# A planned attention and FFN kernel: weight differences and some products and casts also allowed on VectorE, and a new order table

## The chip, the cores and the metric

One core of a Trainium2 chip runs the kernel. The metric is the device time of one execution in microseconds, and lower is better. Before the change three timed runs gave 291.61, 292.24 and 292.89 us, a median of 292.24 us. Engines are called by the profile's names: PE is TensorE, DVE is VectorE, ACT is ScalarE, POOL is GpSimd, and SP is SyncE, which here only issues transfers.

## The reference

Linear attention with exponential features runs on 8 batches of 8 heads (576 tokens, head dimension 64, 128 features), and a maxout FFN takes its output as 4608 tokens of 512 columns.

```python
proj = einsum('bhsd,df->bhsf', x, w_phi)                 # for q and for k
proj = proj - max(abs(proj), axis=-1, keepdims=True)
phi  = concatenate([exp(proj), exp(-proj)], axis=-1)
kv   = einsum('bhsf,bhsd->bhfd', phi(k), v);  z = sum(phi(k), axis=2)
attn = einsum('bhsf,bhfd->bhsd', phi(q), kv) / (phi(q) . z + 1e-6)
x    = attn.transpose(0, 2, 1, 3).reshape(4608, 512)
out  = maximum(maximum(x @ w1, x @ w2), x @ w3) @ w_out
```

## The kernel before

**Units.** The attention is cut into 16 units (half a batch, four heads each). For a unit POOL issues the loads of q (L373) and k (L378) into a `qk_bf` buffer as bf16, and SP those of v (L413) and of the last 64 q tokens of each head, the tail (L405). POOL casts the tail into the same buffer (L408). Units 0 to 3 are transposed by PE; from unit 4 on SP issues two transposing transfers `qkT<-qk_bf` (L454), one for q (8 blocks) and one for k with the tail (10 blocks). PE projects (L474, L572, L579), DVE takes the maxima (L478), ACT the exponentials (L482, L563, L582). POOL multiplies v with a correction from the maxima into `vab` (L527), PE sums `kvps` (L546), PE forms `psn` (L603, L608), DVE adds the two halves into `y` (L614, L617) and takes the reciprocal of the last column (L619), and POOL multiplies the two into `x_sb` (L620, three pieces a unit). From unit 2 on SP issues one transposing transfer `xT<-x_sb` (L639) per unit, and units 0 and 1 are turned by PE (L632).

**FFN.** Nine chunks of 512 tokens follow the units: chunk b needs the turned x of units 2b and 2b+1, the last chunk the tails of all units. The kernel computes max(xw1, xw2, xw3) w_out as max(0, x(w2-w1), x(w3-w1)) w_out plus x(w1 w_out). For this, six weight differences (L739, three column pieces of each of two matrices, `dst - w_bf[0]`, 128x1024 bf16) are made once, and the product w1 w_out is made by PE into `pm` (L760). A chunk then has 12 groups of four products `ups` (L660), ReLU by ACT or DVE (L673, L675), the maximum by DVE (L669), and four row blocks `ops` of four products x(w1 w_out) (L692) and six with `hT` (L697), copied by ACT or DVE (L705) and stored by SP or ACT (L709).

**The order.** Nothing decides the order at run time. Each piece of work is a node with its engine's cost, made in the order of the program text, and the string PLAN lists all 1562 nodes as `number engine buffer-slots @ start`. `plan` gives each node that engine, those slots and that place; `fill` sorts by start and puts products with no use (`idler`, L802) into PE's early gaps. Each engine then works strictly in its order, and SP's and POOL's queues do so too: a transfer that waits holds up all that its engine issues after it. Transfers issued by SP and ACT use eight semaphores in turn, so one waits until the one eight places ahead of it has landed. The cost of a node names the engines on which the planner may put it.

Of the kernel before, what the change touches and what calls it, by code (L numbers as in the profile page):

```python
# [19 lines left out]
P = 128  # L20
# [14 lines left out]
BY_PE = 4  # L35
# [54 lines left out]
109T0@9.7 24T5@10.2 48D@10.4 192G@10.8 21D@10.7 46A@11.3 129T74@10.5 30T23@11.2 110D@11.0 45A@11.5 133D1@11.6 31A@11.8 32A@12.3 115T60@11.8  # L90
120A1@12.7 337S0@8.8 189G@11.0 62G0@11.8 36D@12.0 25D@12.5 33D@12.9 119A1@13.2 1163G@11.9 49T14@13.0 51D@13.5 61G@12.7 35A@13.7 60G@13.7
265G@14.8 122T52@13.6 125D1@14.1 34A@14.2 121D@14.7 55A@14.7 66T43@14.9 57G@15.1 1166G@16.2 50D@15.3 117A@14.9 130A@15.3 56G@16.9 118D@15.9
132D@16.5 127A@15.6 126A@16.1 123A@16.5 82A0@17.0 128D@16.8 131A@17.1 124A@17.4 1165G@18.0 58G@18.8 144A1@17.9 271T0@15.6 140A@18.1 146G1@18.9
272D2@17.4 116A@18.3 267T1@16.0 147G@20.0 69T27@17.6 268D@17.6 143G@20.1 262G@20.3 67D0@18.2 142G@21.0 72A@18.7 335G0@22.1 141G@22.8 79T0@17.9
73A@19.2 280T51@18.3 68D@18.4 71A@19.7 286D0@18.8 111T4@18.7 63T36@19.2 112D@19.4 1164G@23.9 134T74@20.1 405G1@24.6 145G@25.4 80A0@20.2 81A@20.4
64A@20.7 70A@20.9 336G@26.5 164T0@20.9 283D@20.0 65A@21.3 135D@20.6 137T37@21.3 136D@21.2 285A0@21.5 198T2@21.6 139D@21.8 199A3@22.0 138D@22.3
88T64@21.9 83T27@22.5 89D0@22.9 284A0@22.2 282A@22.7 166A1@23.2 165A@23.4 84D1@23.4 196T1@22.9 281A@23.7 154T36@23.6 158A1@24.2 156A@24.7 90D@23.9
157A1@25.1 93T02@24.0 85D@24.4 94D2@24.8 167A1@25.6 1177T5@24.5 194T4@25.0 155A@25.7 148T70@25.5 1178D0@25.3 95D@25.9 159T65@26.1 195A@26.2 161A@27.1
91D0@26.3 86D1@26.4 87G0@27.2 1173T3@26.4 150A1@27.6 149D@26.5 162A@27.7 197D@26.7 92G@27.9 338G@28.7 1174D@27.3 96D2@27.9 151T27@27.0 273T41@27.6
153A@28.2 276D@28.0 152A@28.4 1175T0@27.9 168T37@28.5 98T2@28.9 1176D@28.6 163A@28.5 169D1@29.2 277A@29.0 100T5@29.2 341S0@33.6 170D@29.8 193S3@34.9  # L100
101D@30.3 1181T0@29.3 97G@28.9 160A@29.5 274A@29.9 173T36@30.6 102T7@31.0 275A@30.4 178T54@31.2 1182A@30.9 279D@30.6 174D0@31.2 99D@31.7 207T03@31.8
171D1@31.9 103A@31.4 278A@31.8 1170G@30.8 287T72@32.1 175D@32.0 212A1@32.2 176D0@32.7 289A@32.7 288A@33.0 1183T1@32.4 209A@33.2 291D0@32.8 179D2@33.1
200T62@33.8 208A1@33.7 408S0@35.5 290D@33.6 211A@34.2 172G1@32.9 183T5@34.1 1179T7@34.3 1184D@33.9 475S1@36.1 201A@34.7 180D@34.5 177G@33.7 204A@35.2
185T1@35.6 210D1@35.0 1171G@34.4 181D2@35.6 269T4@35.8 182G@36.5 213D@35.7 202A@35.6 184D@36.3 1168G@37.3 1185T0@36.2 186D@36.6 205A@36.1 270A@36.6
187T3@37.5 1167G@39.4 1186A@37.7 206D@36.8 305T51@37.8 203D@37.4 214T24@38.0 307A0@38.2 188D@38.0 306A0@38.7 219T60@38.4 217D@38.3 1205T3@38.7 308A@39.2
406S2@37.6 1180D@38.7 309A@39.7 220D1@39.3 221D@39.9 1193T5@39.6 218D@40.5 298A0@40.1 225A1@40.3 340S@41.6 266S1@44.4 228A0@40.5 339S2@45.0 1194A1@40.6
216A@41.1 1206D@41.3 1195T7@40.4 222T61@41.4 215A@41.4 224D@41.9 237T04@41.6 1169G@41.5 295T52@41.8 240A1@42.0 1172G@43.6 239A1@42.5 227G@45.7 407G@47.8
238A@43.0 297D@42.5 1207T3@42.2 241A@43.5 301A1@43.9 296D@43.1 1191T1@43.0 1199T2@43.9 1196A@44.1 1192A@44.5 226G@48.0 223D@43.7 310T05@44.8 232T46@45.1
1208D@44.7 292T71@45.3 404G@50.1 311A@45.3 293D@45.7 473G3@50.8 312A@45.7 294D@46.3 1197T3@45.6 235A@46.2 1189T0@46.5 1190D@47.5 233A@46.7 314A@47.2
318A0@47.7 236A@47.8 245A1@48.2 1200A@48.3 242T7@47.3 1198D@48.1 1211T1@47.4 1212D@49.0 1203T0@48.3 1201T6@49.2 300G@51.5 234A@48.8 356T32@50.1 313A@49.3  # L110
# [142 lines left out]
def kernel(  # L253
# [480 lines left out]
    for i in range(2):  # L734
        for h in range(JT // 2):
            c = slice(2 * P * h, 2 * P * (h + 1))
            def diff(n_, i=i, c=c):
                dst = w_bf[i + 1]
                nc.gpsimd.tensor_tensor(dst[:, :, c], dst[:, :, c], w_bf[0][:, :, c], ALU.subtract)  # L739
            n_ = node("wd", 0, {"POOL": 2.1}, None, [w_nodes[0], w_nodes[i + 1]], [], port=True)  # L740
            diffs[i].append([chosen(n_, diff)])
# [92 lines left out]
```

## Time and profile before

| what | value |
|---|---|
| median of three timed runs | 292.24 us (291.61 to 292.89) |
| the profiled execution | 290.7 us |
| its span, first to last instruction | 288.7 us |
| PE busy | 272.4 us, 94% |
| DVE, ACT, POOL busy | 210.6, 199.2, 157.3 us |
| bytes moved | 44.06 MB |

PE counts as busy while a product is under way. Its clock is the share of full speed that it was granted. "issue" as a cause of a wait means that nothing in the profile explains it, and a chain row gives start, duration and work of one piece of the chain that ended last. A row of the timeline ends with the idle time ahead of it and what ended that.

### The profile page before, as it was taken

How to read it: one execution, taken by the hardware profiler on the slowest of the kernel's cores; microseconds unless marked ns; L12 is line 12 of the kernel's file. 1: busy time of each engine (PE TensorE's matmuls, PEld its weight loads, DVE VectorE, ACT ScalarE, POOL GpSimd, SP SyncE). 2: the span in 40 equal slices, each digit the busy share in tenths (PEclk: the TensorE clock that was granted, in tenths of full speed). 3: DMA queues.
4: the chain of work that ended last, by engine and by line, in shares of the span. 5: the costliest groups of instructions: out<-in, count | busy, mean ns of one | idle time of the engine just before them, and what ended most of it. 6: DMA issues, size and time to landing. Idle time of an engine off the chain costs nothing.

```text
span 288.7 us, 8420 instructions
## 1 busy us (share of the span) xinstructions
PE 272.4 (94%) x3432; PEld 150.8 (52%) x3432; DVE 210.6 (73%) x428; ACT 199.2 (69%) x472; POOL 157.3 (54%) x171
## 2 busy tenths in 40 slices
PE   8879999999997949999999999999998999999993
PEld 5557654665554524564555655565455544444541
DVE  3999988999987864885999869989977513155510
ACT  4899999898996773689997998897876220321010
POOL 5699999999726960495178349361982500000000
PEclk9999999999999996999999999999999999999999
DMA  7999999999999999979906399996152330120234
GB/s 161 281 202 209 208 258 258 154 218 154 191 185 232 240 162 283 156 166 182 166 5 167 60 155 242 170 199 141 37 120 86 97 85 0 39 109 36 52 132 109
DMA packets 74678, 44.06 MB, mean 153 GB/s; under 512 B 51152, under 2 KB 65808, under 8 KB 74640
## 3 DMA queue, kind: packets, MB, share of 16 engines
q1 hardware_dynamic: 57296, 27.37, 45.9%
q0 software_dynamic: 14912, 11.77, 28.9%
q10 hardware_dynamic: 2432, 4.39, 4.1%
q8 instruction: 27, 0.44, 0.6%
q14 instruction: 11, 0.09, 0.1%
HBM read 34.64 MB, written 9.44 MB: 153 GB/s over the span
## 4 chain that ended last, share of the span: by engine, by line
PE 72%; DMA 12%; POOL 7%; ACT 3%; issue 2%; SPq 1%; DVE 1%; POOLq 0%; DVEq 0%; ACTq 0%
PE ups L660 30%; PE ops L697 14%; PE ops L692 10%; PE kvps L546 5%; PE psn L603 5%; DMA xT<-x_sb 4%; DMA v_raw<-in_v_dram 3%; POOL vab L527 3%; DMA qkT<-qk_bf 3%; PE psk L474 2%; PE psm L572 2%; DMA tail_raw<-in_q_dram 2%; PE psq L474 2%; ACT Ek L482 2%; PE psn L608 1%
## 5 line engine op out<-in xcount | busy, mean ns | idle before, releaser
L660 PE MATMUL ups<-xT,w_bf 128*128 128x512 bf16 x432 | 104.0, 385 | 4.2 <-DMA xT<-x_sb 4.2
L527 POOL TENSOR_TENSOR vab<-v_raw,em 128x1152 bf16<-128x1152 f32 (+1 forms) x36 | 68.7, 1911 | 22.3 <-DMA qkT<-qk_bf 8.3
L482 ACT ACTIVATE Ek<-psk 128x512 bf16<-128x512 f32 x128 | 73.9, 640 | 6.3 <-PE psk L474 4.0
L563 ACT ACTIVATE Eq<-psm 128x512 bf16<-128x512 f32 x128 | 71.7, 630 | 7.5 <-PE psm L572 6.2
L660 PEld LDWEIGHTS <-w_bf 128*128 128x128 bf16 x432 | 40.1, 99 | 49.6 <-issue 7.2
L620 POOL TENSOR_TENSOR x_sb<-y,rden 128x384 bf16<-128x384 f32 x48 | 38.9, 824 | 38.9 <-DVE rden L619 28.6
L697 PE MATMUL ops<-wout_bf,hT 128*128 128x512 bf16 (+2 forms) x222 | 52.0, 373 | 0.0
L669 DVE TENSOR_TENSOR hT<-hT,ups 128x512 bf16<-128x512 bf16 x54 | 35.5, 681 | 17.1 <-PE ups L660 15.8
L478 DVE TENSOR_REDUCE mk<-psk 128x4 f32<-128x512 f32 x64 | 42.6, 681 | 4.5 <-PE psk L474 2.1
L478 DVE TENSOR_REDUCE mq<-psq 128x4 f32<-128x512 f32 x64 | 41.5, 683 | 4.5 <-PE psq L474 4.3
L673 ACT ACTIVATE hT<-ups 128x512 bf16<-128x512 f32 x40 | 24.9, 634 | 23.6 <-PE ups L660 21.9
L705 ACT COPY osb<-ops 128x512 f32<-128x512 f32 x23 | 13.6, 596 | 37.0 <-PE ops L697 37.0
L697 PEld LDWEIGHTS <-hT 128*128 128x128 bf16 x222 | 20.7, 98 | 22.8
L614 DVE TENSOR_TENSOR y<-psn,sq 128x390 f32<-128x390 f32 x48 | 26.3, 556 | 4.4 <-PE psn L603 2.2
L617 DVE TENSOR_TENSOR y<-y,psn 128x390 f32<-128x390 f32 x48 | 26.3, 556 | 2.4 <-DVE y L614 0.5
L474 PEld LDWEIGHTS <-qkT 64*128 64x128 bf16 x576 | 18.8, 94 | 16.4 <-issue 11.1
L603 PEld LDWEIGHTS <-Eq 128*128 128x128 bf16 x512 | 21.9, 98 | 10.4 <-issue 3.1
L603 PE MATMUL psn<-kv_sb,Eq 128*128 128x65 bf16 x512 | 24.1, 194 | 1.9 <-issue 1.8
L692 PE MATMUL ops<-xT 128*128 128x512 bf16 x96 | 24.6, 380 | 0.0
L675 DVE TENSOR_SCALAR hT<-ups 128x512 bf16<-128x512 f32 x14 | 9.3, 685 | 20.7 <-PE ups L660 20.7
L546 PE MATMUL kvps<-vab,Ek 64*128 64x65 bf16 x1152 | 21.8, 191 | 1.7 <-issue 1.2
L546 PEld LDWEIGHTS <-Ek 64*128 64x128 bf16 x1152 | 20.3, 95 | 2.9 <-issue 1.4
(70 smaller groups left out, 280.6 us busy)
## 6 DMA issues: line engine op xcount, KB each, us to landing
v_raw<-in_v_dram SPq DMA_DIRECT2D x14, 576.0 KB, 6.2
out_dram<-osb SPq DMA_DIRECT2D x20, 256.0 KB, 3.6
qk_bf<-in_k_dram POOLq DMA_DIRECT2D x15, 288.0 KB, 6.6
qk_bf<-in_q_dram POOLq DMA_DIRECT2D x15, 256.0 KB, 6.6
out_dram<-osb ACTq DMA_DIRECT2D x12, 256.0 KB, 2.4
w_bf<-in_moe_w_dram POOLq DMA_DIRECT2D x3, 768.0 KB, 11.6
v_raw<-in_v_dram ACTq DMA_DIRECT2D x2, 576.0 KB, 6.7
tail_raw<-in_q_dram SPq DMA_DIRECT2D x32, 32.0 KB, 5.3
```

Source lines behind the costliest of these rows:

```text
L474: nc.tensor.matmul(ps[s]()[:, i, :], lhsT=qkT()[r, n, :], rhs=wph[r, :], start=True, stop=True)
L478: return nd(kind, {"DVE": 0.598 if n == 4 else 0.331}, lambda: nc.vector.tensor_reduce(dst(m()), ps()[:, 0:n, :].rearrange("p (a j) f -> p ...
L482: return nd("ek", {"ACT": 0.478 if n == 4 else 0.264}, lambda: nc.scalar.activation(dst(Ek[g]()), ps()[:, 0:n, :], EXP, scale=1.0 - 2.0 * ...
L527: made.append(chosen(n_, lambda n_, g=g, t0=t0, t1=t1: (nc.vector if n_.eng == "DVE" else nc.gpsimd).tensor_tensor(vab()[:, g, t0:t1, 0:D] ...
L546: nc.tensor.matmul(kvps[ab]()[:, pr, g, :], lhsT=Ek[g]()[r, t, :], rhs=vab()[r, g, t, :], start=(pr == prs[0] and g + j == 0), stop=(pr == ...
L563: return nd("eq", {"ACT": 0.478 if n == 4 else 0.264}, lambda: nc.scalar.activation(Eq[g]()[:, t0:t0 + n, :], ps()[:, 0:n, :], EXP, scale= ...
L603: nc.tensor.matmul(o, lhsT=Eq[g]()[:, 8 * (c % 2) + 4 * pr + 2 * ab + c // 2, :], rhs=kv()[:, pr, ab, g, :], start=True, stop=True)
L620: divs.append(nd("x", {"POOL": 0.767}, lambda th=th, y=y, rden=rden: nc.gpsimd.tensor_tensor(x_sb()[:, 6 * th:6 * th + 6, :], y()[:, :, 0: ...
L660: nc.tensor.matmul(ups(), lhsT=w_bf[i + (not plain)][:, ct, j * P:(j + 1) * P], rhs=tokens_of(ct), start=(ct == 0), stop=(ct == CT - 1))
L669: nc.vector.tensor_tensor(dst, dst, src, ALU.max)
L692: nc.tensor.matmul(ops_()[:, 0:hi - lo], lhsT=tile_of(ct, tt), rhs=line_w(c_i > MOVE, ct, lo, hi), start=(ct == 0), stop=False)
L697: nc.tensor.matmul(ops_()[:, 0:hi - lo], lhsT=hT()[:, j, tt * P:(tt + 1) * P], rhs=wout_bf[:, j, lo:hi], start=plain and j == 0, stop=(j = ...
```

## The change

Four kinds of nodes may now stand on another engine, and the table is a new one: the planner that made it weighed each order also in two cases in which transfers take longer. The table has the same 1562 nodes. Of what is newly allowed it uses this: two of the six weight differences, three of 48 multiplications into `x_sb` (two of unit 1, one of unit 3) and two of 16 casts of tails go from POOL to DVE. All 36 products of v stay on POOL. Several nodes that had a choice of engine already also change sides: 21 instead of 14 ReLUs and 21 instead of 16 copies of `kvps` are on DVE, 12 instead of 7 small casts L531 and all four copies of `pm` are on ACT. PE has the same products, and 46 instead of 44 idlers. New line numbers lie two or three above the old ones from L527 on.

```diff
 PLAN = """
-14S0@0.8 1D@0.8 3G@1.2 0G@1.6 4A@1.1 5A@1.8 10G0@2.2 16D@4.0 15A@4.0 11S@1.3 ...
...
-        n_ = nd("C", {"POOL": 0.233}, None, [n_t], [t_raw, qk_b], port=True)
+        n_ = nd("C", {"POOL": 0.24, "DVE": 0.13, "ACT": 0.17} if by_pe else {"POOL": 0.24}, None, [n_t], [t_raw, qk_b], port=True)
...
                 costs = {"POOL": 0.128 + 0.1074 * (t1 - t0)}
+                if u < BY_PE:
+                    costs["DVE"] = 0.064 + 0.0667 * (t1 - t0)
...
-            divs.append(nd("x", {"POOL": 0.767}, lambda th=th, y=y, rden=rden: nc.gpsimd.tensor_tensor(
+            n_ = nd("x", {"POOL": 0.767, "DVE": 0.464} if by_pe else {"POOL": 0.767}, None, [n_], [y, rden, x_sb], port=True)
+            divs.append(chosen(n_, lambda n_, th=th, y=y, rden=rden: (nc.vector if n_.eng == "DVE" else nc.gpsimd).tensor_tensor(
...
-                nc.gpsimd.tensor_tensor(dst[:, :, c], dst[:, :, c], w_bf[0][:, :, c], ALU.subtract)
-            n_ = node("wd", 0, {"POOL": 2.1}, None, [w_nodes[0], w_nodes[i + 1]], [], port=True)
+                (nc.vector if n_.eng == "DVE" else nc.gpsimd).tensor_tensor(dst[:, :, c], dst[:, :, c], w_bf[0][:, :, c], ALU.subtract)
+            n_ = node("wd", 0, {"POOL": 2.1, "DVE": 0.64}, None, [w_nodes[0], w_nodes[i + 1]], [], port=True)
```

**SP, around the turning of x of units 4 and 5.** In the rows of before, `qk_bf_1429` belongs to unit 7, `qk_bf_1716` to unit 8, `qk_bf_1949` to unit 9, `x_sb_1999` to unit 4 and `x_sb_2275` to unit 5; a block of 8x128 is q, one of 10x128 is k.

```order
L454 DMA_TRANSPOSE qkT_1697<-qk_bf_1429 128x10x128
L709 DMA out_0_dram<-osb_1752 128x512
L413 DMA v_raw_1961<-in_v_dram 128x2x576
L709 DMA out_0_dram<-osb_1693 128x512
L454 DMA_TRANSPOSE qkT_1983<-qk_bf_1716 128x8x128
L709 DMA out_0_dram<-osb_1427 128x512
L413 DMA v_raw_2063<-in_v_dram 128x2x576
L454 DMA_TRANSPOSE qkT_2142<-qk_bf_1949 128x10x128
L454 DMA_TRANSPOSE qkT_1983<-qk_bf_1716 128x10x128
L413 DMA v_raw_2266<-in_v_dram 128x2x576
L639 DMA_TRANSPOSE xT_75<-x_sb_1999 128x9x128
L639 DMA_TRANSPOSE xT_75<-x_sb_2275 128x9x128
```

After the change, on the same stretch of SP, unit 7 is `qk_bf_1049`, unit 8 `qk_bf_1718`, unit 9 `qk_bf_1810`, and the x of units 4 and 5 are `x_sb_2133` and `x_sb_2295`.

```order
L454 DMA_TRANSPOSE qkT_1920<-qk_bf_1718 128x8x128
L454 DMA_TRANSPOSE qkT_1380<-qk_bf_1049 128x10x128
L413 DMA v_raw_2010<-in_v_dram 128x2x576
L711 DMA out_0_dram<-osb_1645 128x512
L454 DMA_TRANSPOSE qkT_2030<-qk_bf_1810 128x8x128
L405 DMA tail_raw_2126<-in_q_dram 64x2x64 x2
L711 DMA out_0_dram<-osb_1664 128x512
L454 DMA_TRANSPOSE qkT_1920<-qk_bf_1718 128x10x128
L454 DMA_TRANSPOSE qkT_2030<-qk_bf_1810 128x10x128
L405 DMA tail_raw_2251<-in_q_dram 64x2x64 x2
L641 DMA_TRANSPOSE xT_75<-x_sb_2133 128x9x128
L641 DMA_TRANSPOSE xT_75<-x_sb_2295 128x9x128
```

Unit 8's q now stands ahead of unit 7's k, unit 9's q has moved up into this stretch, and of three v loads one is left.

**POOL, the loads in the same stretch.** `qk_bf_2465` is unit 11, `qk_bf_2495` unit 12, `qk_bf_1869` unit 10, and `x_sb_2275` unit 5, in the rows of before.

```order
L620 TENSOR_TENSOR x_sb_2275<-y_2185,rden_2261 128x384
L620 TENSOR_TENSOR x_sb_2275<-y_2218,rden_2284 128x384
L620 TENSOR_TENSOR x_sb_2275<-y_2258,rden_2286 128x384
L527 TENSOR_TENSOR vab_2215<-v_raw_1431,em_2204 128x18x64
L378 DMA qk_bf_1869<-in_k_dram 128x2x576
L527 TENSOR_TENSOR vab_2368<-v_raw_1961,em_2348 128x18x64
L373 DMA qk_bf_2465<-in_q_dram 128x4x256
L373 DMA qk_bf_1949<-in_q_dram 128x4x256
L378 DMA qk_bf_2495<-in_k_dram 128x2x576
```

After the change `x_sb_2295` is unit 5, `tail_raw_2251` the tail of unit 10, and `qk_bf_2406`, `qk_bf_2443` and `qk_bf_2461` are units 10, 12 and 11.

```order
L529 TENSOR_TENSOR vab_2185<-v_raw_1495,em_2176 128x18x64
L533 CAST vab_2185<-em_2176 128x36
L623 TENSOR_TENSOR x_sb_2295<-y_2262,rden_2280 128x384
L623 TENSOR_TENSOR x_sb_2295<-y_2229,rden_2293 128x384
L623 TENSOR_TENSOR x_sb_2295<-y_2174,rden_2316 128x384
L408 CAST qk_bf_2406<-tail_raw_2251 128x2x64
L378 DMA qk_bf_2406<-in_k_dram 128x2x576
L373 DMA qk_bf_2406<-in_q_dram 128x4x256
L378 DMA qk_bf_2443<-in_k_dram 128x2x576
L373 DMA qk_bf_2461<-in_q_dram 128x4x256
```

The second product of v of unit 6 now stands ahead of x of unit 5 instead of behind it. All loads behind x wait for a cast, and the cast for the tail that SP issues just ahead of x. Unit 9's q load has left this stretch.

**POOL, the loads ahead of unit 7's k transposition.** In the rows of before the loads are those of unit 7's k, unit 8's q, unit 10's q, unit 8's k and unit 9's k.

```order
L378 DMA qk_bf_1429<-in_k_dram 128x2x576
L527 TENSOR_TENSOR vab_1734<-v_raw_980,em_1728 128x18x64
L373 DMA qk_bf_1716<-in_q_dram 128x4x256
L373 DMA qk_bf_1869<-in_q_dram 128x4x256
L378 DMA qk_bf_1716<-in_k_dram 128x2x576
L378 DMA qk_bf_1949<-in_k_dram 128x2x576
```

After the change five loads stand behind one another.

```order
L373 DMA qk_bf_1718<-in_q_dram 128x4x256
L378 DMA qk_bf_1049<-in_k_dram 128x2x576
L373 DMA qk_bf_1810<-in_q_dram 128x4x256
L378 DMA qk_bf_1810<-in_k_dram 128x2x576
L378 DMA qk_bf_1718<-in_k_dram 128x2x576
```

Unit 10's q load has left this place, and unit 9's q load has come to it. Unit 7's k is now second in the row, behind unit 8's q.

More of the change, by code (lines that the diff above doesn't have):

```diff
@@ L90 @@
[L90 to L93, printed above, removed]
@@ L196 @@
[L196 to L197 removed]
+11S0@0.8 1D@0.8 4A@1.1 0G@1.2 14S@1.3 3G@1.7 5A@1.8 17S0@1.9 9G0@2.2 2G@2.9 105G1@3.1 106S1@3.5 104G@3.8 12A@4.0
+7A@4.3 13A@4.6 6A@4.9 191S2@5.1 20T0@5.1 21D0@5.8 30T12@6.3 337S3@6.7 34A0@6.7 33D0@6.7 15A@7.2 16D@7.3 31A@7.5 36D@7.5
```

221 lines of the change are left out of this document (111 added, 110 removed).

## The prediction

> **What bounds the kernel now.** I read the page first (busy time, slices, chain by engine), then windows of one slice each.
>
> ```profile
> PE 272.4 (94%) x3432; PEld 150.8 (52%) x3432; DVE 210.6 (73%) x428; ACT 199.2 (69%) x472; POOL 157.3 (54%) x171
> PE   8879999999997949999999999999998999999993
> PEclk9999999999999996999999999999999999999999
> PE 72%; DMA 12%; POOL 7%; ACT 3%; issue 2%; SPq 1%; DVE 1%; POOLq 0%; DVEq 0%; ACTq 0%
> 86.40:93.60 7.20, 5.47 (x58) 2.95 (x58) 5.24 (x14) 4.88 (x13) 4.62 (x5) 1.00 1.31 242
> 100.80:108.00 7.20, 3.67 (x62) 2.26 (x59) 4.54 (x11) 6.01 (x14) 4.66 (x6) 0.94 1.53 157
> 108.00:115.20 7.20, 6.53 (x98) 3.18 (x99) 2.85 (x6) 2.06 (x5) 0.21 (x1) 0.59 1.18 285
> 216.00:223.20 7.20, 5.95 (x90) 3.76 (x84) 5.24 (x13) 4.36 (x13) 1.47 (x3) 1.00 0.20 75
> ```
>
> PE has no gap from about 30 us to the end but for three holes. In a window row the first pair is PE's busy time, and behind the five pairs come the granted clock and DMA's share. The holes lie at 86 to 94, 101 to 115 and 216 to 223 us; in the middle one the clock falls to 0.59. PE's work is the same before and after, so the change can pay only in these holes and lose only by new ones or a later start. All else PE hides.
>
> The chain of waits through the middle hole, with a row of full speed from further on:
>
> ```profile
> 76.83 9.48 DMA v_raw<-in_v_dram
> 86.38 2.13 POOL vab L527
> 88.51 1.28 SPq L454
> 89.89 7.90 DMA qkT<-qk_bf
> 97.88 10.75 DMA xT<-x_sb
> 108.67 4.42 PE ups L660 x10
> 169.65 3.45 PE ups L660 x16
> ```
>
> PE stood still before the first products of chunk 2, which need x of units 4 and 5, and the transfer of unit 5 was issued at 97.88 us and took 10.75. Then ten products took 4.42 us; at 3.45/16 = 0.216 each they take 2.16.
>
> ```profile
> L660 PE MATMUL ups<-xT,w_bf 128*128 128x512 bf16 x432 | 104.0, 385 | 4.2 <-DMA xT<-x_sb 4.2
> L572 PE MATMUL psm<-qkT,wph 64*128 64x512 bf16 x2 | 0.6, 604 | 0.0
> DMA to landing us min/median/max: 3.2/3.5/10.8
> ```
>
> **Hole 1, worth 6.8 us**: 4.2 of wait, 4.42 - 2.16 = 2.26 of slow products, and some 0.3 for the other products that the slow clock caught (two took 604 ns each). The median landing of such a transfer is 3.5 us, the largest is this one.
>
> ```profile
> 88.13 0.22 PE L603 MATMUL psn<-kv_sb,Eq 128*128 128x65 bf16 x2 [1.81 <-issue]
> 217.34 0.23 PE L546 MATMUL kvps<-vab,Ek 64*128 64x65 bf16 x3 [1.25 <-issue]
> q8 instruction: 27, 0.44, 0.6%
> ```
>
> **Holes 2 and 3, 1.81 and 1.25 us**, stand inside a node (ahead of the last two of twelve `psn` products, of the last three of 72 `kvps` products), where no data can be missing. The profile names no releaser. The instruction queue q8 has 27 transfers, one per 254 of PE's 2 x 3432 loads and products, so I take these for late instructions: once behind full DMA queues (share 1.31), once in a dense run, where two sums `kvps` follow each other.
>
> **Why the x transfer was late**, from the timelines of SP and POOL:
>
> ```profile
> 73.67 1.61 SPq L454 DMA_TRANSPOSE qkT<-qk_bf  x1
> 78.74 6.17 SPq L454 DMA_TRANSPOSE qkT<-qk_bf  x1
> 87.20 6.83 SPq L454 DMA_TRANSPOSE qkT<-qk_bf  x2
> 96.08 5.25 SPq L639 DMA_TRANSPOSE xT<-x_sb  x2
> L639 SPq DMA_TRANSPOSE xT<-x_sb x14: 1242/1306/3448, 62.1 to 230.6; - x14
> 86.38 2.12 POOL L527 TENSOR_TENSOR vab<-v_raw,em 128x1152 bf16<-128x1152 f32 x1 [5.17 <-DMA v_raw<-in_v_dram]
> 95.53 0.76 POOL L378 DMA_DIRECT2D qk_bf<-in_k_dram  x1
> 98.66 1.55 POOL L373 DMA_DIRECT2D qk_bf<-in_q_dram  x2
> 100.19 0.72 POOL L378 DMA_DIRECT2D qk_bf<-in_k_dram  x1
> ```
>
> SP was held at its transposing transfers (6.17 and 6.83 us; the median of a turning's issue is 1.31), and once x of unit 5 was out, four loads of POOL, issued from 95.53 to 100.91, moved beside it.
>
> **The change part by part.**
>
> *(a) The order of transfers around x of units 4 and 5: -6.8 us.* After the change the four loads behind x stand behind a cast that needs the tail of unit 10, and SP issues that tail just ahead of x. So they cannot start early; unit 9's q load, one of the four, has left, and unit 10's q load, which had left the front, has come instead. Unit 7's product of v, which led up to them, no longer stands between. The second product of v of unit 6, which stood between x of unit 5 and the loads, now stands ahead of x: 2.13 us, the vab row of the chain. POOL has room for it: it waited 5.17 us for v just before. What must come true is little: at the same issue, the transfer is in time at 10.75 - 4.2 = 6.5 us, against a median of 3.5. Above, SP is held no less than before: it has one transposition more ahead of x and two v loads fewer. Bounds: 0, if transfer and issue are as late as now, and -6.8, if both are as the median has it. I take -6.8, the end that the median is nearer to.
>
> ```profile
> v_raw<-in_v_dram SPq DMA_DIRECT2D x14, 576.0 KB, 6.2
> ```
>
> Late next is unit 7's v load, which SP now issues behind x of unit 5 (it stood nine places ahead of it): some 1.3 us of issue, 6.2 to landing and two products of 2.13 are 11.8 us to its `kvps`, less the 3.5 to 6.5 us that x is under way when chunk 2 begins. That leaves 5.3 to 8.3 us, in which PE has chunk 2's first groups and projections to do; its price is in rival 1.
>
> *(b) Hole 2: -0.9 us.* Whether an instruction block is late depends on DMA traffic about 7 us ahead of its use. The traffic there changes, but does not become small. Bounds -1.81 and 0, and I take the middle, having no row nearer. The Trainium skill (Runtime: NRT & Kernel Launch, section Instruction fetch mechanics) says that crossing an instruction block is mostly hidden. By that rule hole 2 was something else, this term is 0 and the time 0.9 us higher; the rows with 1.81 and 1.25 us inside a node do not agree with it.
>
> *(c) Hole 3: 0.* Units 14 and 15 still have their `kvps` one behind the other. Bounds -1.25 and +1.25.
>
> *(d) Differences, x and casts on DVE, and the front: +1.0 us.*
>
> ```profile
> L739 POOL TENSOR_TENSOR w_bf<-w_bf x6: 2117/2126/2129, 31.0 to 44.1; 128x1024 bf16<-128x1024 bf16 x6
> L753 DVE COPY hT<-pwT 128x1024 bf16<-128x1024 bf16 x3 | 2.0, 681 | 0.0
> L669 DVE TENSOR_TENSOR hT<-hT,ups 128x512 bf16<-128x512 bf16 x54 | 35.5, 681 | 17.1 <-PE ups L660 15.8 <-ACT hT L673 0.8
> L620 POOL TENSOR_TENSOR x_sb<-y,rden 128x384 bf16<-128x384 f32 x48 | 38.9, 824 | 38.9 <-DVE rden L619 28.6 <-issue 6.3 <-DMA qkT<-qk_bf 3.9
> L617 DVE TENSOR_TENSOR y<-y,psn 128x390 f32<-128x390 f32 x48 | 26.3, 556 | 2.4 <-DVE y L614 0.5
> L660 PE MATMUL ups<-xT,w_bf x432: 377/379/631, 39.8 to 270.9; 128*128 128x512 bf16 x144
> L802 PE MATMUL idler<-idle 128*128 128x256 bf16 x44 | 8.6, 322 | 1.2 <-DVE idle L328 1.1
> ```
>
> POOL gives up 2 x 2.13 + 3 x 0.82 = 6.7 us and two casts. DVE takes two differences, each between 0.68 (a copy of the same size) and 1.36 (twice the two-operand row of half the size), and three x at about 0.56: 3.0 to 4.4 us. `ups` waited for x alone (the 4.2 above), never for a difference, so earlier differences gain nothing: the lower bound is 0. DVE is behind ACT's and PE's work there with idle time of its own. What can cost is a difference that now waits behind DVE's maxima: at most one old difference exposed, 2.13 us. Two more idlers in PE's early gaps (0.64 us of filling) say that the front is somewhat looser. I take the middle, 1.0.
>
> *(e) The other nodes with a new side* (ReLUs, copies): DVE at 73% and ACT at 69% are not on the path but by PE's waits: 0, with the cover that PE always has a product ready.
>
> Sum: -6.8 - 0.9 + 1.0 = -6.7. The profiled execution, 288.7 + 2.0 around its span = 290.7, becomes 284.0. It lies 1.5 below the median of the timed runs, 292.24, so I carry the difference over: 292.24 - 6.7 = 285.5 us.
>
> **The rivals.**
>
> *1. x comes late again, but less.* SP is in order and as full as before, and the transfer of unit 5, or behind it the v load of unit 7, then misses by about 2 us (the 8.3 above against some 6 of work). A wait of 1.81 us did not lower the clock (1.00 in the window at 86.40), so only those 2.0 are lost: 287.5.
>
> *2. The change does not do what it says.* The hole stays whole, because the transposing transfers hold SP as now: 285.5 + 6.8 = 292.3, no change that can be measured. For it: SP's 6.17 and 6.83. Against: the loads behind x are chained to x's own neighbour.
>
> *3. Slower: unit 7's k transposition.*
>
> ```profile
> qkT<-qk_bf SPq DMA_TRANSPOSE x1, 10.6
> 89.88 0.28 PE L474 MATMUL pst<-wph,qkT 64*128 64x128 bf16 x4
> ```
>
> It was issued at 73.67 and landed 10.6 us later, at 84.3; PE began unit 7's projections at 89.88, of which 1.81 was hole 2. So it has 89.88 - 84.3 - 1.8 = 3.8 us to spare. Now unit 8's q stands ahead of it on SP, and five loads in a row ahead on POOL. If it lands over 3.8 us later, PE waits; if it is later by another 4, as in the present hole, the clock falls too. Price: a hole like the present one, 6.8, and x 2.0 late behind it on the same queue: 285.5 + 6.8 + 2.0 = 294.3. For it: one transposition behind another was held 6.17 us. Against: in the table of before it was also among four loads.
>
> *4. DVE and POOL block each other.* Two differences and three x on DVE read two operands from SBUF; before, DVE's large two-operand work (L614, L617, L669) always read one from PSUM. If such an instruction waits for a POOL one, a difference comes 2.13 us later, and so may the first `ups`: 287.6. The Trainium skill (SBUF — State Buffer, section Who interferes with whom) says exactly this of VectorE instructions with two SBUF inputs against GpSimd ones that read SBUF; no run here shows it yet.
>
> **How the numbers follow.** The forecast of 285.5 has a chance of 0.50, rival 1 of 0.17, rival 2 of 0.13, rival 3 of 0.16, rival 4 of 0.04. About 0.5% (1.5 us) is what a measurement of this kernel can tell from no change. Faster by more: 0.50 + 0.17 + 0.04 = 0.71; same 0.13; slower 0.16. The range is 283.4 to 293.8: the low end is the forecast with hole 2 and 3 both gone (-0.9, -1.2), the high end takes in rival 2 with the full front of (d), and leaves out more than half of rival 3. The forecast's own range is 283.4 to 287.
>
> **What would show it.** (a) is right if no wait of `ups` for xT over 1 us remains and the clock stays at 1.00 from 30 us to the end; if it stays below 1 in a slice, rival 2 or 3 holds, and the chain says by `xT` or by `qkT` ahead of `psk`, `pst` or `psq`. (b) shows as "issue" waits of PE inside a node near 88 us, (c) near 217 us. (d) shows as waits of `pm` or `ups` for differences or copies between 27 and 50 us, or a first `ups` after 40.8 instead of 39.8; rival 4 as DVE differences over 1.4 us. The prediction is wrong if PE has a new hole elsewhere, most likely before the `kvps` of unit 7.

## The result and the profile after

| | before | after |
|---|---|---|
| median of 15 timed runs | 291.15 us (289.43 to 295.10) | 291.23 us (290.08 to 309.77) |
| ratio after/before | | 0.9998, 95% interval 0.9972 to 1.0025 |
| profiled execution, span | 290.7, 288.7 us | 290.72, 288.6 us |

No difference that can be measured; 285.5 us had been forecast. Two of the 15 runs after the change lie at 306.79 and 309.77 us, and the runs of some kernels below also fall into two groups: all ratios compare the lower group alone.

The page after the change, the same rows as before: busy time, PE's slices, its clock, and the chain by engine.

```profile
PE 271.3 (94%) x3434; PEld 150.0 (52%) x3434; DVE 219.3 (76%) x439; ACT 198.8 (69%) x473; POOL 150.7 (52%) x159
PE   7697988999996899999999999999999999999994
PEclk9979999999999999999999999999999999999999
PE 66%; DMA 10%; DVE 9%; ACT 6%; issue 4%; POOL 3%; SPq 1%; ACTq 0%; POOLq 0%; DVEq 0%
```

The middle hole with its half clock and the hole near the end are gone. In their place stand a looser front (the first seven slices) and a new hole in slices 13 and 14. DVE, which had 1% of the chain before, has 9% of it. The windows of the three old holes and of the new one:

```profile
36.00:43.20 7.20, 5.77 (x68) 3.08 (x65) 7.19 (x14) 5.45 (x13) 7.19 (x7) 1.00 1.17 250
86.40:93.60 7.20, 4.50 (x84) 2.69 (x76) 4.70 (x9) 5.68 (x15) 5.67 (x6) 1.00 1.20 124
93.60:100.80 7.20, 6.13 (x61) 3.06 (x62) 4.84 (x11) 2.56 (x6) 3.83 (x5) 1.00 1.29 253
108.00:115.20 7.20, 7.20 (x75) 3.72 (x74) 6.60 (x15) 6.20 (x17) 5.16 (x6) 1.00 1.15 202
216.00:223.20 7.20, 7.20 (x195) 4.64 (x193) 6.19 (x12) 5.59 (x12) 1.48 (x2) 1.00 0.11 39
```

PE is full at 108 and at 216 us, where it was not, and short at 36 and at 86 to 101 us, where the window at 36 had been full (7.08 us busy before). What it waits for now (total, times, longest):

```profile
PE psk L474 <- DMA qkT<-qk_bf: 3.5, 1, 3.5
PE psn L605 <- issue: 1.4, 1, 1.4
PE pxT L634 <- DVE x_sb L623: 1.2, 2, 0.8
PE ups L662 <- DVE w_bf L741: 0.3, 1, 0.3
PE ups L662 <- DMA xT<-x_sb: 0.2, 1, 0.2
```

The 4.2 us for xT have become 0.2 (at chunk 3; there is none at chunk 2). New are 3.5 us for a transposition, 1.2 us for x made by DVE, and 1.4 us inside a row of `psn` products for which no releaser is seen.

**Lost time by work done.** Two spans of the same length hide what happened, since a hole early in one moves all that follows. So I compared the kernels at equal work of PE. For each group of products the trace gives its start and that of the next one; the usual step of a group of its kind, the same for all kernels, is its work, and the time on the clock minus the work done so far is lost time. With another choice of the usual step most of the differences between the kernels move by some tenths, up to about half a us.

| us of PE's work done | 5 | 15 | 30 | 60 | 65 | 80 | 85 | 180 | 190 |
|---|---|---|---|---|---|---|---|---|---|
| before | 12.0 | 16.6 | 18.3 | 20.3 | 20.5 | 23.4 | 30.5 | 34.7 | 36.2 |
| after | 14.4 | 17.7 | 21.9 | 24.2 | 24.4 | 31.0 | 31.2 | 35.9 | 36.1 |
| `loads_q9` | 12.1 | 17.2 | 19.1 | 21.0 | 21.2 | 23.3 | 25.2 | 29.3 | 30.8 |
| `v11_k7_x_pool` | 14.6 | 18.0 | 20.3 | 22.6 | 22.8 | 24.0 | 25.7 | 30.7 | 30.9 |

After against before, column to column: the front loses 3.9 us more (0 to 60), the stretch with hole 2 and the new hole 3.7 more (65 to 80), that of hole 1 loses 6.9 less (80 to 85), the long middle 0.5 more, and that of hole 3 loses 1.3 less (180 to 190). The sum is -0.1, the difference of the spans. So a gain of the expected size came and was given back in two places. The experiments are about these two places, and about hole 1 by itself. In their edits, `617S1@73.7` is node 617 on SP, with buffer slot 1, at 73.7 in the table; slot numbers that are only written at another node of the same buffer are left out.

### The profile page after: what moved, and what is told of

The parts are those of the page before. It is cut to its first block, busy times and chain, and to the rows that moved or that the text cites. A ratio compares the mean times of both kernels' runs of the same rounds, so it can differ in the third digit from the quotient of the medians.

```text
span 288.6 us, 8418 instructions
## 1 busy us (share of the span) xinstructions
PE 271.3 (94%) x3434; PEld 150.0 (52%) x3434; DVE 219.3 (76%) x439; ACT 198.8 (69%) x473; POOL 150.7 (52%) x159
## 4 chain that ended last, share of the span: by engine, by line
PE 66%; DMA 10%; DVE 9%; ACT 6%; issue 4%; POOL 3%; SPq 1%; ACTq 0%; POOLq 0%; DVEq 0%
PE ups L662 24%; PE ops L699 14%; PE ops L694 9%; DMA qkT<-qk_bf 8%; PE psn L605 5%; PE kvps L548 4%; DVE mk L478 3%; PE psq L474 2%; DVE mq L478 2%; ACT Eq L565 2%; PE psm L574 2%; ACT Ek L482 2%; PE psk L474 2%; SPq L454 1%; DMA xT<-x_sb 1%
## 5 line engine op out<-in xcount | busy, mean ns | idle before, releaser
L662 PE MATMUL ups<-xT,w_bf 128*128 128x512 bf16 x432 | 102.3, 379 | 1.1 <-DVE w_bf L741 0.3
L482 ACT ACTIVATE Ek<-psk 128x512 bf16<-128x512 f32 x128 | 72.9, 626 | 9.1 <-PE psk L474 6.0
L529 POOL TENSOR_TENSOR vab<-v_raw,em 128x1152 bf16<-128x1152 f32 (+1 forms) x36 | 68.3, 1917 | 18.3 <-issue 10.6
L662 PEld LDWEIGHTS <-w_bf 128*128 128x128 bf16 x432 | 39.4, 98 | 45.7 <-issue 2.5
L623 POOL TENSOR_TENSOR x_sb<-y,rden 128x384 bf16<-128x384 f32 x45 | 36.6, 824 | 46.0 <-DVE rden L621 39.7
L707 ACT COPY osb<-ops 128x512 f32<-128x512 f32 (+1 forms) x24 | 14.2, 592 | 39.1 <-PE ops L699 35.4
L675 ACT ACTIVATE hT<-ups 128x512 bf16<-128x512 f32 x33 | 20.2, 618 | 21.0 <-PE ups L662 21.0
L699 PEld LDWEIGHTS <-hT 128*128 128x128 bf16 x222 | 20.3, 98 | 21.7
L474 PEld LDWEIGHTS <-qkT 64*128 64x128 bf16 x576 | 18.3, 95 | 18.7 <-issue 10.9
L605 PE MATMUL psn<-kv_sb,Eq 128*128 128x65 bf16 x512 | 24.2, 194 | 1.4 <-issue 1.4
L707 DVE COPY osb<-ops 128x512 f32<-128x512 f32 (+1 forms) x13 | 8.7, 677 | 14.5 <-PE ops L699 14.4
```

The source lines that it names most:

```text
L474: nc.tensor.matmul(ps[s]()[:, i, :], lhsT=qkT()[r, n, :], rhs=wph[r, :], start=True, stop=True)
L482: return nd("ek", {"ACT": 0.478 if n == 4 else 0.264}, lambda: nc.scalar.activation(dst(Ek[g]()), ps()[:, 0:n, :], EXP, scale=1.0 - 2.0 * ...
L529: made.append(chosen(n_, lambda n_, g=g, t0=t0, t1=t1: (nc.vector if n_.eng == "DVE" else nc.gpsimd).tensor_tensor(vab()[:, g, t0:t1, 0:D] ...
L605: nc.tensor.matmul(o, lhsT=Eq[g]()[:, 8 * (c % 2) + 4 * pr + 2 * ab + c // 2, :], rhs=kv()[:, pr, ab, g, :], start=True, stop=True)
L623: divs.append(chosen(n_, lambda n_, th=th, y=y, rden=rden: (nc.vector if n_.eng == "DVE" else nc.gpsimd).tensor_tensor(x_sb()[:, 6 * th:6 ...
L662: nc.tensor.matmul(ups(), lhsT=w_bf[i + (not plain)][:, ct, j * P:(j + 1) * P], rhs=tokens_of(ct), start=(ct == 0), stop=(ct == CT - 1))
```

## Experiments: the late k

The chain through the new hole, after the change:

```profile
73.21 0.70 POOL qk_bf L378
73.91 0.76 POOL qk_bf L373
74.67 1.41 POOL qk_bf L378 x2
80.39 13.93 DMA qkT<-qk_bf
94.37 0.44 PE psk L474 x8
```

Four loads of POOL (the last four of five in a row), then a transposition of 13.93 us from issue to landing: unit 7's k, as rival 3 had it. On SP it stood in this row (three transpositions, the k being the third), and ACT's queue put a load of v beside it (at 80.32; the 80.65 that an expectation below names is ACT's next instruction):

```profile
71.93 14.37 SPq L454 DMA_TRANSPOSE qkT<-qk_bf  x3
80.32 0.43 ACTq L413 DMA_DIRECT2D v_raw<-in_v_dram  x1
```

**The k ahead on SP.** In the kernels of the first four runs (`k7_first`, `unit9_late`, `loads_behind_x5`, `moves_alone`) line numbers are 44 higher than otherwise, since the table takes more lines.

```diff
-617S1@73.7 547S@75.2
+547S@73.65 617S1@73.7
```

> The changed kernel with one edit: on SP the transposition of unit 7's k stands ahead of unit 8's q instead of behind it. Theory A (place on SP): the k landed at 94.32 because it was issued as the second of two transposing transfers; issued first at about 80.4 it lands as in the kernel before, some 9 us later, at about 89.5, and PE, which is ready for it at 90.9, does not wait. The 3.5 us of wait and the 2 to 3 us that follow while unit 7 catches up go: 285 to 286.5 us. Theory B (traffic: five loads of POOL just ahead and transfers of v beside it): the k still lands after 93, the wait stays at 2 us or more, and the time is 289 to 291.

Measured: 287.93, 288.09, 292.26 and 305.06 us; ratio 0.9882 (0.9801 to 0.9962) by the first two. The profiled run is that of 305.06 us. In it the k was issued first, at 95.99, and landed at 108.73, 12.74 us later instead of 13.93, and PE waited 2.0 us instead of 3.5. By this profile the place on SP is worth 1.4 us of issue (in the changed kernel unit 8's q stood 1.37 us ahead of the k, at 79.02) and 1.2 us of landing, some 2.6 in all: theory A, which gave it nearly 5 us, falls as stated, and traffic is the larger part of the landing. In time the two short runs lie 3 us under the changed kernel's median; no profile of such a run was kept.

**Less traffic ahead of the k.**

```diff
-680G1@69.5 681G@70.2 686S0@80.3 685S@85.8
+681G@84.0 685S0@92.65 680G@92.7 686S@104.95
```

> The changed kernel with the order on SP of unit 8's q ahead of unit 7's k kept, but unit 9's two loads and its two transpositions put off until behind the turning of x of units 4 and 5, so that three loads instead of five stand ahead of the k. Theory A (place on SP): the k still lands after 92 and the wait of PE for it stays above 1.5 us, 289 to 291. Theory B (traffic): with two loads of 256 to 288 KB less the k lands by 91, the wait goes, 285 to 286.5.

Measured: 301.11, 302.24, 317.70 and 318.76 us, ratio 1.035 (1.0264 to 1.0437). As to the k, theory B holds: unit 8's q landed 4.4 us after the start of its issue, the k 6.5 us after (81.55 to 88.06), and no wait for it is left. The time rose by two other waits. ACT, about to issue its v load, was held for a store of output to land:

```profile
90.07 0.46 ACTq L457 DMA_DIRECT2D v_raw<-in_v_dram  x1
90.58 0.60 ACT L526 ACTIVATE Ek<-psk 128x512 bf16<-128x512 f32 x1 [8.05 <-DMA out_dram<-osb]
```

PE lost 6.6 us to that, as the transfers of SP and ACT share eight semaphores in turn and the edit had changed whose turn it was (the store, issued by SP at 84.11, landed at 90.05 and freed the semaphore that ACT's load needed); and 5.4 us to unit 7's v, behind the moved transpositions on SP. With the v load of ACT held back too, this run does not say which of the transfers mattered.

**One v load elsewhere.** The next three stand on a front with the five operations back on POOL, where no run goes above 295 us:

```diff
-177D@34.6 182D@36.1 1167D@38.9 1169D@43.2 333D@65.5
+177G@34.6 182G@36.1 1167G@38.9 1169G@43.2 333G@65.5
```

> The changed kernel with the three multiplications into x and the two weight differences back on POOL, at their places in time; all else as changed. Theory A (an operation of DVE with two operands in SBUF waits while POOL works: x took 0.99 and 1.47 us, a difference 1.54 us and in one run 10.31 us beside POOL, 0.68 us while POOL stood still): the waits of pxT for x on DVE (1.2 us) and of ups for w_bf on DVE go, 1.5 to 2.5 of the 3.9 us lost in the front come back, 288.5 to 290 us, and no run goes above 300 us. Theory B (the new order of the front is itself later, and POOL has no room): the front loses as much, 291 us or more.

Measured: 292.96 us, ten runs from 291.62 to 294.16, ratio 1.0045 (1.0015 to 1.0076). Theory B: the waits for x and for differences on DVE went, but differences on POOL now came late.

```profile
PE psk L474 <- DMA qkT<-qk_bf: 2.8, 1, 2.8
PE ups L662 <- POOL w_bf L741: 2.8, 2, 1.8
```

Then the v load of unit 11 alone, moved from ACT to SP behind x of unit 5:

```diff
-822A1@76.4
+822S1@95.0
```

> The kernel of front_pool with one edit: the load of unit 11's v, 576 KB, which ACT issued at 80.65 beside the transposition of unit 7's k and which is needed after 150 us only, is issued by SP behind x of unit 5. Theory traffic: the k lands some 3 us earlier, by 91, and at most 2 us of the 3.5 us of wait at psk are left: 1.5 to 4 us under front_pool. Theory place (the k is late because it stands second on SP): the wait stays at 3 us or more and the time within 1 us of front_pool.

Measured: 287.97, 288.24, 288.33 and 293.82 us, ratio 0.9882 (0.9835 to 0.9930) by the first three, 4.7 us under `front_pool`. The k's place, first in `front_pool` and then without the v load:

```profile
96.28 0.40 PE L474 MATMUL psk<-wph,qkT 64*128 64x128 bf16 x8 [2.82 <-DMA qkT<-qk_bf]
```
```profile
92.33 0.40 PE L474 MATMUL psk<-wph,qkT 64*128 64x128 bf16 x8
```

The k landed 8.55 us after its issue began (82.08 to 90.63) instead of 13.19 (83.05 to 96.24). One load of 576 KB, which POOL needed only at 147.63 after the change, made the difference, with the order on SP and all five loads as they were. In the profiled run, that of 293.82 us, x came late in turn: PE waited 5.3 us for it, beside the v load that now stands behind it.

> The kernel of front_pool_v11 with unit 7's k also ahead of unit 8's q on SP. Both theories of the late k: it lands by 90. If PE still waits at this psk, the wait is not for the k but for instructions (the place is the 2499th instruction of PE, where the kernel before had its hole of 1.81 us too), it then ends over 1 us after the k has landed, and is 1 to 2 us long. 285 to 287.5 us.

Measured: 288.23 us (287.37 to 289.45), ratio 0.9887 (0.9835 to 0.9939): the same as without the k ahead, and no wait for transposed data in the list at all. With the v load gone the place on SP gained no further time.

## Experiments: hole 1

```diff
-818G2@94.8 680G@95.6 888G0@96.3 887G@99.2 819G@102.4 686S@104.9
+819G2@102.4 680G@102.45 818G@102.5 888G0@102.55 887G@102.6 686S@104.9
```

> The table of before with one edit: the four loads that POOL issued beside x of unit 5 (q of units 9, 11 and 12, k of unit 12) stand behind the next load on POOL, some 6 us later. Theory A (the loads beside x made it late): x lands by 104, the wait of ups for xT is under 0.5 us and the clock stays at 1.00, 284 to 285.5 us. Rival (SP's transposing transfers hold x whatever moves beside it): the wait stays at 3 us or more, 290 to 291.5.

Measured: 285.46, 285.98, 287.10, 291.92 and 292.42 us; ratio 0.9803 (0.9723 to 0.9883) for the first three. x of unit 5 took 7.01 us instead of 10.75 and hole 1 is 1.2 instead of 7.1 us of lost time: theory A. But in the profiled run, that of 292.42 us, the next x was late (5.1 us of wait):

```profile
98.30 7.01 DMA xT<-x_sb
...
127.30 7.72 DMA xT<-x_sb
```

Unit 9's q, now among the last of five loads, landed at 119.26; its transposition waited for it at the head of SP, and x of units 6 and 7 stood behind that. So with the q left beside x, and an edit for hole 3:

```diff
-818G2@94.8 888G0@96.3 887G@99.2 1130T63@203.1 1132D1@204.5 1131A@205.4 1422T@206.6
+818G@102.5 888G0@102.55 887G@102.6 1130T63@205.6 1422T@205.7 1132D1@205.78 1131A@205.79
```

> The table of before with three of the four loads behind x of unit 5 (q of unit 9, which the order on SP needs first, stays), and kvps of unit 15 no longer directly behind that of unit 14: a turn of projections and one row block ops stand between. Theory A for the loads: the wait of ups for xT is 1.5 us or less, the clock stays at 1.00, and no other x is late: 284 to 286 us. Rival: the one load left is enough, hole of 3 us or more, 290 to 291.5. For the hole of 1.25 us inside kvps: if instructions come late because 288 of them are used up in 2.4 us, it shrinks to under 0.6; if it has another cause it stays.

Measured: 290.17 us (288.50 to 291.56), ratio 0.9951 (0.9916 to 0.9986). With one load left beside x, x of unit 5 took 8.46 us, and the stretch has 3.2 us of wait (in two pieces, 1.7 the longer) and 5.4 us of lost time. The wait inside kvps went; the stretch did not gain by it (2.0 us lost from 180 to 190, 1.5 before), since products behind it now waited for `y` and `osb` on DVE. Now all four loads behind x again, with the q first among them and its transposition moved too, and without the edit for hole 3 (the lines for the other three loads are as above):

```diff
-680G@95.6 686S@104.9
+680G@101.65 686S@112.25
```

> The table of before with only the transfers around x of units 4 and 5 put in another order: the four loads behind x of unit 5, unit 9's q first among them, and unit 9's q transposition behind x of unit 6 instead of ahead of it on SP. Theory A (hole 1 is a matter of the loads beside x; put off with their users it leaves no new hole): wait of ups for xT under 1 us in both chunks, clock 1.00 from 30 us on, 284 to 286 us. Rival (what is put off always collides with the next x): a hole of 3 us or more at chunk 3, 289 to 291.

Measured: **285.35 us**, six runs from 283.31 to 287.04, ratio 0.9805 (0.9757 to 0.9853), without any of the changed kernel's edits. x of unit 5 took 6.38 us, and no later x made PE wait. Its waits:

```profile
PE ups L660 <- DMA xT<-x_sb: 1.4, 2, 1.0
PE kvps L546 <- issue: 1.2, 1, 1.2
```

## Experiments: the front

The operations that went to DVE, after the change, and POOL's in the same stretch:

```profile
36.52 0.99 DVE L623 TENSOR_TENSOR x_sb<-y,rden 128x384 bf16<-128x384 f32 x1
38.43 1.47 DVE L623 TENSOR_TENSOR x_sb<-y,rden 128x384 bf16<-128x384 f32 x1
42.15 1.54 DVE L741 TENSOR_TENSOR w_bf<-w_bf 128x1024 bf16<-128x1024 bf16 x1
47.26 0.68 DVE L741 TENSOR_TENSOR w_bf<-w_bf 128x1024 bf16<-128x1024 bf16 x1
```
```profile
40.99 2.14 POOL L741 TENSOR_TENSOR w_bf<-w_bf 128x1024 bf16<-128x1024 bf16 x1
43.06 0.74 POOL L378 DMA_DIRECT2D qk_bf<-in_k_dram  x1
46.95 0.34 POOL L533 CAST vab<-em 128x36 bf16<-128x36 f32 x1 [3.15 <-ACT em L521]
```

A difference of the same size took 0.68 us while POOL stood still and 1.54 us when it was called during POOL's of 2.14 us. The moves alone, in the table of before (with the changed program text, which lets them stand on DVE):

```diff
-192G@10.8 265G@14.8 177G@33.7 182G@36.5 1167G@39.4 1169G@41.5 333G0@61.7
+192D@10.8 265D@14.8 177D@33.7 182D@36.5 1167D@39.4 1169D@41.5 333D0@61.7
```

> The table of before with one part of the change alone: the two weight differences, three multiplications into x and two casts of tails go from POOL to DVE at the places in time that they had. The changed kernel has lost 3.9 us more than the one before by 60 us of PE's work. Theory A (the operations on DVE delay PE): most of it is seen here, 2 to 4 us lost by then, 293 to 295 us. Theory B (the new order of the front, which the planner itself put 1.1 us later at 45 us): under 1 us of it is seen here, 290.5 to 292.

Measured: 298.94 us (296.41 to 302.29), ratio 1.0228 (1.0135 to 1.0320). Theory A, and more of it: in the profiled run, the longest (302.29 us), 27.6 us were lost by 60 us of work instead of 20.3, and the stretch of hole 1 lost 12.8 instead of 7.1. In the order of before the moves do harm; how they enlarge hole 1 was not followed. That the new order is built around them may be why `front_pool` lost 2.6 us more than the changed kernel and not less.

Next, the two edits for the late k on the changed front:

> The changed kernel with the two edits that removed the late k (v of unit 11 behind x of unit 5, unit 7's k ahead of unit 8's q on SP), its front as changed, with the differences and x on DVE. If the late k and what followed it are worth what the place showed (6.2 us of lost time between 65 and 80 us of PE's work, against 1.1 to 1.4 without it), 286 to 287 us; if the front of the changed kernel and not the late k ate the gain, 289.5 or more. Single runs above 300 us stay possible, since a difference on DVE can still wait for all that POOL has in a row.

Measured: 284.98 and 286.15 us, and 301.33, 302.00, 303.65 and 309.08 us; ratio 0.9814 (0.9753 to 0.9875) by the first two. In these two of six runs the changed kernel without the late k has its gain. The profiled run is that of 302.00 us, and it shows, like that of `k7_first`, what makes the long ones: in both a difference on DVE took over 10 us (10.34 and 10.31). DVE and POOL in `k7_first`:

```profile
52.41 10.31 DVE L785 TENSOR_TENSOR w_bf<-w_bf 128x1024 bf16<-128x1024 bf16 x1
```
```profile
51.98 0.76 POOL L417 DMA_DIRECT2D qk_bf<-in_q_dram  x1
52.75 4.21 POOL L573 TENSOR_TENSOR vab<-v_raw,em 128x1152 bf16<-128x1152 f32 x2
56.90 0.28 POOL L452 CAST qk_bf<-tail_raw 128x128 bf16<-128x128 f32 x1
57.14 0.81 POOL L417 DMA_DIRECT2D qk_bf<-in_q_dram  x1
57.96 4.20 POOL L573 TENSOR_TENSOR vab<-v_raw,em 128x1152 bf16<-128x1152 f32 x2
62.10 0.76 POOL L452 CAST qk_bf<-tail_raw 128x128 bf16<-128x128 f32 x1
```

A difference of 0.68 us lasted 10.31 us, until POOL had gone through four products of v in a row, and PE stood 9.8 us for it. Its turn came with POOL's last cast, which took 0.76 us where another took 0.28. Is it this one instruction? Its return to POOL alone:

```diff
-1169D@43.2
+1169G@43.2
```

> The kernel of v11_k7 with one edit: the second of its two weight differences on DVE, the one that took 10.3 us in the profiled run, goes back to POOL. If the runs of 301 to 309 us (four of six of v11_k7) are this one difference, waiting until POOL has nothing left in a row, no run goes above 295, and the time is that of the good runs of v11_k7 (285.0 and 286.2) plus 0 to 2 us for a later w_bf. If they come from something else (x on DVE, ACT, transfers), a part of the runs stays above 300.

Measured: 288.30 us, twelve runs from 286.54 to 294.09, ratio 0.9888 (0.9858 to 0.9918). None goes above 300 us any more, where four of six did. The price is 2.6 us of wait for the difference on POOL. And x back on POOL, both differences on DVE:

```diff
-177D@34.6 182D@36.1 333D@65.5
+177G@34.6 182G@36.1 333G@65.5
```

> The kernel of v11_k7 with the three multiplications into x back on POOL, the two differences left on DVE. With both on POOL the front lost 2.6 us more than with both on DVE. If x on DVE is what the front gains by (pxT waits 1.2 us as it is), taking it back costs 1 to 2 us more; if only the differences gain (2.8 us of waits for w_bf on POOL without them), the front loses 1 us less than that of v11_k7.

Measured: 285.57 us (284.28 to 286.52), ratio 0.9811 (0.9766 to 0.9856). The second expectation, and beyond it: the front lost 22.6 us by 60 instead of 24.2 in the changed kernel, both differences took 0.68 to 0.70 us, and none of the four runs goes above 287 us (few, where the long ones come at random). So by one profile of each, x on DVE cost the changed front 1.6 of its 3.9 us.

## Experiments: waits without a releaser

The hole of 1.81 us before, that of 1.25 and the one of 1.36 us in the front after the change stand ahead of PE's 2498th, 6083rd and 706th instruction (products, weight loads and its few semaphore instructions counted, 4 to 14 up to these places). Each number is 194 or 195 above a multiple of 256. To move the numbers and nothing else:

```diff
-            nc.tensor.matmul(idler[:, 0:2 * P], lhsT=idle, rhs=idle.unsqueeze(1).to_broadcast([P, 2, P]), start=True, stop=True)
+            for c in (slice(0, P), slice(P, 2 * P)): nc.tensor.matmul(idler[:, c], lhsT=idle, rhs=idle, start=True, stop=True)
```

> The kernel before with each product without use as two of half the width, so that every later instruction of PE has a number 88 higher. If the holes of 1.81 and 1.25 us are late blocks of 256 instructions, their place moves by 88 instructions: none at the psn products at about 88 us, and inside kvps of unit 15 with 47 products left to do instead of 3. If they hang on the place in the program (a conflict, the data or the traffic at that point), they stay at the last two psn and the last three kvps. The time is 290 to 292 in either case.

Measured: 289.74 us, ten runs from 283.49 to 293.75; the ratio of 0.9754 (0.9695 to 0.9814) goes by the two shortest runs, 283.49 and 284.94, alone. Hole 1 is whole in the profiled run (5.8 us of wait at 289.14 us); the two shortest suggest that it does not come in every run, but neither was profiled. Both waits are gone: `psn` at 86 to 88 us runs through, and so do both sums of kvps.

```profile
213.55 2.47 PE L546 MATMUL kvps<-vab,Ek 64*128 64x65 bf16 x144
```

The new hole foretold inside kvps did not open, so the number alone does not make a hole. Nor does it elsewhere: `loads_q9` runs through the 2498th instruction without a wait, and after the change the 6083rd stands in the same `kvps`, 13 products before the end, without one. The same edit on two other kernels:

> The kernel of v11_k7_x_pool with each product without use as two of half the width, so that later instructions of PE have a number 92 higher. If the 1.5 us ahead of psn at about 28.4 us (PE's 706th instruction) are a late instruction block, they go, and the front loses 1 to 1.5 us less; elsewhere such a hole may open. If they hang on the place, they stay.

Measured: **283.28 us** (282.14 to 284.28), ratio 0.9725 (0.9684 to 0.9765), the best of all. The 1.48 us at 28.42 in `v11_k7_x_pool`, first fence, are gone in the second:

```profile
26.19 0.75 PE L605 MATMUL psn<-kv_sb,Eq 128*128 128x65 bf16 x18
28.42 0.35 PE L605 MATMUL psn<-kv_sb,Eq 128*128 128x65 bf16 x6 [1.48 <-issue]
```
```profile
26.15 0.93 PE L605 MATMUL psn<-kv_sb,Eq 128*128 128x65 bf16 x24
```

> The kernel of loads_q9 with each product without use as two of half the width, as in idlers_split, where the holes inside psn and kvps had gone. If those were late instruction blocks and the transfers stay as in loads_q9, the 1.18 us inside kvps go: 283.5 to 285 us. If the edits disturb each other (other start times, x late again), 287 or more.

Measured: 285.02 us (280.94 to 286.44), ratio 0.9731 (0.9670 to 0.9792); the wait in kvps is gone, but in the profiled run, the longest of the six, a transposition came 2.5 us late. Against `loads_q9` no clear gain.

**The packets.** What the number alone does not say, the packets of the instruction queue q8 do: 27 in each profile, of 16 KB each, against 27 blocks of 256 in PE's 6883 instructions. The kept traces have their times; "place" is the number of the instruction at which PE came to the next packet's block.

| kernel, place | PE reached it | packet for it moved | PE went on |
|---|---|---|---|
| before, 2498 | 86.13 | 85.70 to 86.65 | 88.13 |
| `loads_q9`, 2498 | 86.84 | 82.34 to 83.66 | at once |
| after, 2498 | 90.71 | 89.50 to 91.53 | 94.37 (unit 7's k landed at 94.32) |
| `k7_first`, 2498 | 106.89 | 106.52 to 107.69 | 109.11 (unit 7's k landed at 108.73) |
| before, 6083 | 215.91 | 215.06 to 215.93 | 217.34 |
| after, 6083 | 219.12 | 215.15 to 216.18 | at once |
| after, 706 | 26.60 | 25.97 to 26.94 | 28.16 |

In the 14 profiles that have all of PE's records, PE came to 17 such places before their packet had ended or less than 0.5 us after. It stood at each of them, and at all but one (2498 after the change) it went on 1.2 to 1.5 us after the packet's end. At the other places, over 300, the packet had ended at least 1.2 us before PE came, and no wait without a releaser of 0.6 us or more stands there. So the holes are late instruction blocks. The table also says that hole 2 is still there after the change, under the wait for unit 7's k: with the k in time PE would have stood there until 1.2 to 1.5 us after 91.53, some 2.0 to 2.3 us. In `k7_first` it was the packet and no longer the k that ended the wait.

## Why the prediction was wrong, point by point

*(a) Hole 1: -6.8.* Right in size (-6.9), and by its own signs: no wait of `ups` for xT over 0.2 us, and a clock of 1.00 from 30 us on. That loads beside x make it late is shown by `loads_behind_x5`, `three_loads_k15` and `loads_q9`. After the change SP issued x of unit 5 at 105.54, POOL the loads only from 107.22, and x landed at 108.79, 2.0 us ahead of the first products that need it (110.77). Part of that may be luck: the hole ahead had made PE some 5 us later by then. In six profiles without the late k, where the v load of unit 11 moves beside x instead, PE waited for x in four (5.3, 1.4, 1.3 and 0.8 us). What the new order alone is worth with PE in time is not shown.

**The step that failed** is the sentence behind (a)'s sum, "Late next is unit 7's v load": late next was unit 7's k, and the sum has no term for it. Rival 3 had the right transfer, with a chance of 0.16, and its 3.8 us to spare were used up: the k landed 10.0 us later than before (94.32 instead of 84.3). It cost less than rival 3's price of 8.8: the stretch from 65 to 80 lost 6.6 us, 2.9 before, of which 1.8 were hole 2. That leaves about 5.5 for the late k, unit 7's catching up and the late block under it, which alone would have taken some 2 us. Rival 3's reason was only half right. The place behind unit 8's q is worth some 2.6 us of the k's arrival. The v load that the new table gave to ACT's queue is worth 4.6 us of landing (13.19 to 8.55) and 4.7 us of time on the front of `front_pool`, and without it the place gained no further time. I had followed SP and POOL around this point, and ACT's queue not at all.

*(b) Hole 2: -0.9.* It seems to have gone whole (-1.8), since no wait without a releaser stands there, but it lies under the wait for the late k, which stood at the very same instruction. *(c) Hole 3: 0.* It went (-1.3), though both sums kept their places: the packet for the 6083rd instruction had ended 2.9 us before PE came. Neither outcome was foretold. That these are late instruction blocks, as the prediction took them, the packet times show. So does its remark on traffic: before, PE passed the place one block ahead of the 2498th instruction at 79.06, 7.1 us earlier, and the packet came 6.6 us after that; in `loads_q9`, with other traffic, it came 2.6 us after it (79.78 to 82.34), and there was no hole. The Trainium skill (Runtime: NRT & Kernel Launch, section Instruction fetch mechanics) gives blocks of 256 instructions, which agrees with the three numbers above, and calls their crossing mostly hidden, which agrees by count; the 17 places that were not hidden cost 0.7 to 2.0 us each where nothing else held PE.

*(d) The front: +1.0.* It was +3.9, and this term was mis-sized by 2.9 us; the first `ups` came at 42.4 instead of 39.8. Shown are 1.6 for x on DVE and 1.4 for an instruction block that now fell into the front. The other 0.9 stay open: the new table itself puts PE's work about 1 us later at 45 us, but the clock was also 0.77 from 14.4 to 21.6 us, where before it was 1.00, and `loads_q9`, which has the front of before and a clock of 0.76 there, lost 0.7 us more than before too. The bound of 2.13 rested on "at most one old difference exposed"; x on DVE, which PE waited for in turning it (pxT), was counted at 0.56 us and took up to 1.47, and 2.38 and 2.73 in the profiled run of `v11_k7`.

*Rival 4, DVE and POOL block each other,* got 0.04, and it is what happens, with a wrong price: I let the instruction wait for one of POOL's (2.13 us), and it can wait for all that POOL has in a row (10.31). The Trainium skill (SBUF — State Buffer, section Who interferes with whom) says that a VectorE instruction with two SBUF inputs contends with GpSimd ones that read SBUF; the rows of 0.68, 1.54 and 10.31 us agree, and maxima with one input kept their 0.68 us beside POOL.

*Slips of the working.* SP's 6.83 us is a row of two transpositions, held 2.60 and 4.14 us. Rival 2 with the full front of (d) is 292.3 + 2.13 - 1.0 = 293.4 us and not 293.8. The measured 291.23 us lies near rival 2's 292.3, but not for its reason: hole 1 went.

*(e)* No wait of note goes back to the ReLUs and copies that changed sides. *Rivals 1 and 2* did not happen in the profiled run.

## What to carry to other kernels

When a new order clears one late transfer, ask of each transfer in that stretch how much time it has to spare, and count all queues that issue there, those of compute engines too: here most of what the late transfer cost came back when one large load, which nobody needed soon, was sent elsewhere. A wait that ends with a transfer can hide another behind it, here a late instruction block. An instruction with two operands in SBUF was cheap on DVE only where POOL paused (0.68 us); its price was not its duration, but up to POOL's whole row of work (10.31 us). Compare two traces at equal work done, not at equal time: here a gain of 8.2 us and losses of 8.1 us gave two spans of one length.

## What was not expected of the hardware

- DVE did not get its turn between two of POOL's instructions: in two profiles it waited through six of them, a transfer's issue included, that followed without a gap (10.31 and 10.34 us).
- PE went on only 1.2 to 1.5 us after the end of an instruction packet that it waited for, at 16 places in 14 profiles.
- A wait of 3.46 us (after) left PE's clock at 1.00 in both windows around it; behind one of 4.20 us (before) it was 0.59.
- A compute engine that issues a transfer can be held by an older transfer of another queue: ACT for 8.05 us.
- A transposing transfer of q or k took between 4 and 14 us from issue to landing, by what else moved: 4.4 and 6.5 us in `unit9_late`, 13.93 us after the change.
- One kernel's runs differ by more than some of the effects here: the kernel before ranges from 289.29 to 296.05 us in one set of 17. Why was not tried.
